# Linear-attention numerators in three head groups instead of four, with inverted gate coefficients and a new instruction order

## The chip, the cores and the metric

The kernel runs on one core of a Trainium2 chip. The core has five engines that run their own instruction streams in order: TensorE (PE, matrix products, with a separate row for its weight loads, PEld), VectorE (DVE), ScalarE (ACT), GpSimd (POOL) and SyncE (SP, which here only issues DMA transfers). Engines wait for one another through semaphores. The metric is the device time of one execution in microseconds (us), as the median of several runs. Products write into PSUM tiles; DVE and ACT read these, POOL works on SBUF alone.

## The reference

One input `x` (2048 rows of 640) goes through two attention layers, A and B, with 32 heads of 20 channels each, and a gate per row mixes them. Everything is in bf16 at the interface.

```python
# A: linear attention; phi(t) = concat(softmax(t), softmax(-t)) over a head's 20 channels
pq = einsum('bhsd,hdf->bhsf', q, w_phi); pk = einsum('bhsd,hdf->bhsf', k, w_phi)
kv = einsum('bhsf,bhsd->bhfd', phi_k, v); z = einsum('bhsf->bhf', phi_k)
num = einsum('bhqf,bhfd->bhqd', phi_q, kv)
den = einsum('bhqf,bhf->bhq', phi_q, z)[..., None] + 1e-06
a = (num / den).reshape(B, S, D) @ wo
# B: four segments of 512 rows; in each, causal softmax attention and a memory M, z of the earlier ones
a_dot = softmax(qs @ ks.T * scale + mask) @ vs
a_mem = (phi(qs) @ M) / (phi(qs) @ z + 1e-06)
o = g * a_mem + (1.0 - g) * a_dot           # g = sigmoid(beta), one per head
M = M + phi(ks).T @ vs; z = z + phi(ks).sum(rows)
b = o_all @ wo_B
# the mix
g = sigmoid((x * gate_w).sum(-1, keepdims=True)); out = g * a + (1 - g) * b
```

Both parts end in a product with 640 x 640 weights, and the gate is one number per row, so the kernel applies the gate to the attention outputs ahead of that product and adds both parts in one accumulation.

## The kernel before

**Tiling.** The 2048 rows are cut into 16 blocks of 128 (a block is the partition dimension) and four segments of 512 rows. The 640 channels are five tiles of 128. Since a head has 20 channels, a tile of 128 rows of a transposed matrix holds 6 or 7 heads and a bit; the tables `H0`, `NH` and `OFF` say which heads touch which of the five tiles.

**PSUM.** One large tile `st4` (four times 512 fp32) holds the attention logits of part B. All other products share four tiles `w` of 512 fp32 a partition. Each use takes a free one (`alloc`), and the last instruction that reads it gives it back (`free`).

**Stages.** The start loads x0 to x3 (the first four row blocks of x), transposes them with PE products (line 681) into `xT` (copied by ACT, line 691, or DVE, line 693) and loads weights. The later blocks of x come by transposing DMAs. Then, for each segment: projections of part B (`seg_in`, line 745: K, Q, V and the gate's logit); K and Q go to DRAM (`kd`, line 764) and come back transposed (`kqT`, line 1109); 20 rounds of logits (line 1138) and one exponential over 128 x 2048 each (line 1144, ACT, tile `PT`), whose diagonal blocks POOL masks (line 1150); products with V (line 1166) and with the memory (line 1185). Part A first goes once over all 16 blocks for its state (`a1`, lines 841 to 867, `kv_pass`, `a1_state`, tile `KVD`). From there on (`switch`, 155 us in the profile) it makes, for each segment, the exponentials of the projected Q with both signs (`a3_pq`, line 988, and the exponentials `Eq`, line 996) and the numerators (`a3_num`). Last, `fin` multiplies both parts' outputs, transposed (`oTA`, `oTB`), with the output weights (line 1086) and stores (`osb`).

**Numerators.** `a3_num(s, qc, hf)` makes half the heads of a row block, in two groups of 8 heads (`PARTS`, indexed by `qt`). A group's products (line 1019) fill 2 x 8 x 22 columns of one tile w: for each sign and head the 20 numerator channels, the product with z (column DH) and the sum of the exponentials (column DH+1, by ones in `KVD`). The two softmaxes are not normalized ahead; with E the numerator, Z its z column and S the sum for either sign, the output is (E1/S1 + E2/S2) / (Z1/S1 + Z2/S2), which is (E1*S2 + E2*S1) / (Z1*S2 + Z2*S1). Six instructions do this, in order: `dz` copies the sums (line 712 on DVE or 710 on ACT), `xx` multiplies Z with the other sign's sum (1032), `rr` adds the two signs (1035) and is inverted (1038), `cs` is the other sign's sum times gate times rr (1040), `ts` scales the numerators (1044) and frees the tile w. Then POOL adds the two signs of a half, 16 heads, into `oA` (1048), and SP stores the row block to DRAM (1054), from where a transposing DMA fetches it for `fin` (1060).

**Output of part B.** `b_out(s, g, ...)` takes four heads' results of a segment. Column DH of the tile w is the denominator; `nx` is 1 in the first segment, where there is no memory part, and 2 in the others. Each part's 16 denominators are inverted (1203) into `rd`, `rd` is multiplied with the coefficients `Cdm` of both parts (1206), and the numerators are scaled by it (1214); POOL adds the parts (1220). `Cdm` is made per segment by POOL (813) from the rows' gates `omgS` (807) and the heads' `omg_b` and `sig_b` (824 to 826).

**Order.** Nothing is scheduled at run time. `ORDER` is a table that lists, for each engine, the numbers of the operations in the order in which the engine gets them; a number is the position at which `op(...)` recorded the operation. (`29*7` stands for 29 to 35.) Operations with two possible engines (`AD`: ACT or DVE, mostly copies out of PSUM) go to the one in whose list they stand. The planner only walks the lists and hands out tiles w; the durations written in `op` serve its walk. `lk=True` marks DVE instructions after which the next POOL instruction gets a wait on that instruction (`run`, "port order").

## Time and profile before

| | us |
|---|---|
| median of 7 runs (lowest 291.19, highest 292.19) | 291.8 |
| the profiled execution | 291.47 |
| its span, first to last instruction | 289.8 |
| PE, ACT, DVE, POOL busy in the span | 281.8, 246.9, 229.3, 188.8 |
| granted TensorE clock | 1.000 |

The busy time by stage, in us:

| stretch | what it mostly holds | PE | DVE | ACT | POOL |
|---|---|---|---|---|---|
| 0 to 20 | loads, transposes, first projections | 18.33 | 9.69 | 8.43 | 8.15 |
| 20 to 40 | projections, first logits | 19.46 | 10.61 | 15.04 | 9.38 |
| 40 to 155 | segments 0 to 2 of B, state of A | 114.77 | 96.12 | 110.24 | 89.58 |
| 155 to 268 | numerators of A, rest of B, output products | 110.50 | 105.12 | 107.75 | 76.66 |
| 268 to 290 | last output products and stores | 18.72 | 7.81 | 5.44 | 4.99 |

PE's busy time counts a product from its start to its modelled end, and products overlap (a 320-column product is shown with 299 ns while the next starts some 136 ns later), so 97% busy is not PE at its peak. The chain of waits is followed back from the last instruction, at each step to what released it. A group of instructions is one line, engine, operation and tile; its row gives the number of instances, the busy time and the mean duration in ns.

### The profile page before, as it was taken

What the parts mean: (1) busy time and instruction counts of PE and PEld (TensorE: products, weight loads), DVE (VectorE), ACT (ScalarE), POOL (GpSimd) and SP (SyncE); (2) the same over time, 40 slices, a digit from 0 to 9 for tenths busy, and PEclk for the clock granted to TensorE, in tenths of its full rate; (3) what the DMA queues carried; (4) which work ended last, traced back from release to release, by engine and by line L of the source; (5) the groups of instructions that cost most, each with busy time, mean ns of one, the idle gap of its engine ahead of it and who ended that gap; (6) DMA issues with size and microseconds to landing.
All of it is one profiled execution on the core that took longest, in us unless ns stands there. A gap on an engine that the chain in (4) does not pass through costs nothing.

```text
span 289.8 us, 9799 instructions
## 1 busy us (share of the span) xinstructions
PE 281.8 (97%) x3764; PEld 192.8 (67%) x3777; DVE 229.3 (79%) x850; ACT 246.9 (85%) x353; POOL 188.8 (65%) x333
## 2 busy tenths in 40 slices
...
GB/s 214 309 214 152 119 248 80 147 106 87 134 42 105 159 102 69 99 57 141 2 125 263 129 181 123 170 79 122 160 171 117 140 105 197 128 100 131 104 106 65
DMA packets 87976, 38.42 MB, mean 133 GB/s; under 512 B 69882, under 2 KB 83834, under 8 KB 87930
## 3 DMA queue, kind: packets, MB, share of 16 engines
...
q10 hardware_dynamic: 656, 0.41, 0.5%
q14 instruction: 17, 0.14, 0.2%
...
## 4 chain that ended last, share of the span: by engine, by line
PE 78%; DVE 14%; DMA 4%; issue 1%; SPq 1%; ACT 1%; POOL 0%; DVEq 0%
PE w L745 34%; PE w L1086 14%; PE w L1166 9%; PE st L1138 7%; PE w L988 4%; DVE ts L1044 4%; PE w L1019 3%; DMA WvA<-in_A_wqkv_dram 2%; PE w L888 2%; DVE cs L1040 2%; PE w L1231 1%; DVE rr L1038 1%; DMA Wc<-in_A_w_phi_dram 1%; DVE tdm L1214 1%; PE w L1185 1%
## 5 line engine op out<-in xcount | busy, mean ns | idle before, releaser
L1144 ACT ACTIVATE PT<-st 128x2048 bf16<-128x2048 f32 x80 | 151.5, 1893 | 4.8 <-PE st L1138 3.8
L1150 POOL TENSOR_SCALAR_AFFINE_SELECT PT<-PT 128x512 bf16<-128x512 bf16 x128 | 79.1, 635 | 42.1 <-ACT PT L1144 13.5
L745 PEld LDWEIGHTS <-xT 128*128 128x128 bf16 x800 | 72.4, 97 | 34.7 <-issue 9.5
L867 POOL TENSOR_TENSOR EkN<-Ek,krec 128x640 bf16<-128x640 bf16 x32 | 40.5, 1273 | 4.6 <-DVE phik L778 1.2
L1166 PEld LDWEIGHTS <-PT 128*128 128x128 bf16 x1280 | 39.8, 96 | 5.3 <-issue 0.8
L1166 PE MATMUL w<-vB,PT 128*128 128x21 bf16 x1280 | 41.5, 172 | 0.1
L745 PE MATMUL w<-WqB,xT 128*128 128x320 bf16 x160 | 36.0, 299 | 0.3 <-ACT kq L710 0.2
L745 PE MATMUL w<-WvA,xT 128*128 128x340 bf16 (+1 forms) x160 | 35.4, 299 | 0.2 <-DMA WvA<-in_A_wqkv_dram 0.2
L745 PE MATMUL w<-WkB,xT 128*128 128x320 bf16 x160 | 34.4, 299 | 0.4 <-DVE xT L693 0.4
L1048 POOL TENSOR_TENSOR oA<-ts 128x320 bf16<-128x320 f32 x32 | 27.4, 862 | 10.9 <-DVE dz L712 3.1
L745 PE MATMUL w<-WkA,xT 128*128 128x320 bf16 x160 | 33.5, 299 | 0.0
L745 PE MATMUL w<-WvB,xT 128*128 128x321 bf16 (+1 forms) x160 | 33.3, 300 | 0.1
L1086 PE MATMUL w<-WoA,oTA 128*128 128x320 bf16 x160 | 32.3, 298 | 0.2
L1086 PE MATMUL w<-WoB,oTB 128*128 128x320 bf16 x160 | 32.3, 299 | 0.0
L1138 PE MATMUL st<-kqT 32*128 32x384 bf16 (+3 forms) x512 | 31.7, 300 | 0.5 <-ACT PT L1144 0.5
L1044 DVE TENSOR_TENSOR ts<-w,cs 128x320 f32<-128x320 f32 x64 | 30.6, 486 | 1.4
L988 PE MATMUL w<-xT,WqA 128*128 128x512 bf16 x87 | 26.7, 378 | 0.8 <-DVE ts L1044 0.2
L1019 PE MATMUL w<-KVD,Eq 128*128 128x88 bf16 (+3 forms) x256 | 26.8, 207 | 0.6
L859 DVE TENSOR_REDUCE ksum<-Ek 128x32 f32<-128x640 bf16 x32 | 25.1, 804 | 2.7 <-ACT Ek L852 2.6
L1220 POOL TENSOR_TENSOR oB<-tdm 128x320 bf16<-128x320 f32 x24 | 20.6, 863 | 7.6 <-DVE dz L712 2.7
L852 ACT ACTIVATE Ek<-w 128x320 bf16<-128x320 f32 x64 | 24.2, 453 | 1.5 <-PE w L745 1.0
L1019 PEld LDWEIGHTS <-Eq 128*128 128x128 bf16 x256 | 19.2, 97 | 9.2 <-issue 2.8
(113 smaller groups left out, 447.7 us busy)
## 6 DMA issues: line engine op xcount, KB each, us to landing
...
```

Of the source, the lines that this page charges most:

```text
L745: nc.tensor.matmul(w[:, 0:width], lhsT=T["xT"][:, c, sc * P:(sc + 1) * P], rhs=T[Wn][:, c, lo:lo + width], start=(c == 0), stop=(c == KC - 1))
L859: op("DVE", 0.74, lambda sgn=sgn: nc.vector.tensor_reduce(out=T["ksum"][js][:, H * sgn:H * sgn + H], in_=T["Ek"][ik][:, sgn].rearrange("p ...
L867: op("POOL", 1.22, lambda sgn=sgn: nc.gpsimd.tensor_tensor(out=T["EkN"][ie][:, 0:2 * D].rearrange("p (h x f) -> p h x f", x=2, f=DH)[:, :, ...
L988: nc.tensor.matmul(w, lhsT=T["WqA"][:, c, t * P:(t + 1) * P], rhs=T["xT"][:, c, s * L:(s + 1) * L], start=(c == 0), stop=(c == KC - 1))
L1019: nc.tensor.matmul(w[:, c0:c0 + m * E2], lhsT=T["Eq"][j][:, sgn, qc * P:(qc + 1) * P], rhs=T["KVD"][:, sgn, OFF[t] + a:OFF[t] + a + m, :]. ...
L1044: op("DVE", dve_t(320), lambda w, c3=c3, qt=qt: nc.vector.tensor_tensor(out=T["ts"][d][:, :, 8 * (qt % 2):8 * (qt % 2) + 8], in0=vw(w)[:, ...
L1048: op("POOL", 0.82, lambda: nc.gpsimd.tensor_tensor(out=T["oA"][o][:, 320 * hf:320 * hf + 320].rearrange("p (h d) -> p h d", d=DH), in0=T[" ...
L1086: nc.tensor.matmul(w[:, 0:320], lhsT=T[nm][j][:, k5, :], rhs=T[Wo][:, k5, hf * 320:hf * 320 + 320], start=(i == 0), stop=(i == 9))
L1138: nc.tensor.matmul(st4[:, i, o:o + w], lhsT=T["kqT"][j][r:r + 32, 0, c * P:(c + 1) * P], rhs=T["kqT"][j][r:r + 32, 1, c * P:L], start=True ...
L1144: op("ACT", act_t(2048), lambda: nc.scalar.activation(out=T["PT"][slot], in_=st4, func=ACT.Exp, scale=SCALE_B), r=("st4",), w=(("PT", slot ...
L1150: nc.gpsimd.affine_select(out=v, in_=v, pattern=[[0, 4], [1, P]], compare_op=ALU.is_ge, fill=0.0, base=0, channel_multiplier=-1)
L1166: nc.tensor.matmul(w[:, j * 84 + i * V1:j * 84 + (i + 1) * V1], lhsT=T["PT"][slot][:, i, o + (j - c) * P:o + (j - c + 1) * P], rhs=T["vB"] ...
```

## The change

- `PARTS` has three groups of 11, 11 and 10 heads (`NHG` = 11). `a3_num` makes groups 0 and 1 with `hf` = 0 and group 2 with `hf` = 1. A group's products fill 484 (or 440) of the 512 columns of a tile w; there are 7 products per sign and row block where there were 8. The six instructions stand once per group. The buffers `dz` to `ts` are three each, one per group; `ts` had two, one per half.
- POOL's addition into `oA` comes after each group, over 11 or 10 heads, not after each half of 16. The store of a row block waits for three additions.
- `omgS`, `omg_b` and `sig_b` become the inverses of what they were, by further reciprocals in `gates` and `beta`, and with them `Cdm`. `b_out` multiplies the denominators in the tile w by `Cdm` first, part by part, and takes one reciprocal over both parts. The multiply no longer carries `lk`.
- `ORDER` is replaced as a whole. On SP the loads of `beta_b` (13) and `Wc` (11) stand right behind the first x block, ahead of the other three; on POOL the mask `m36` (operation 42) stands ahead of the identity (26). The numbers shift, since there are fewer operations.

```diff
@@ ORDER (first lines of each list)
     "PE":
-        "29*7 73*3 77*2 80 88 104 89 82 120 90*2 105 121 92 106 94 122 95 107 123 96 108 124 126 "
...
+        "29*7 73*3 77*2 80 88*2 82 90 104*2 91 106*3 120 92 110*2 121*2 94 112 123*2 113 142 114 "
...
     "ACT":
-        "0 76 79 28 86 101 109 99 133 147 149 197 117 213 229 205 189 175 221 237 187 266 367 431 "
-        "405 510 252 513 245 279 268 287 399 291 315 299 666 843 307 517 379*2 386*2 528 418 411 "
...
+        "0 28 86 79 81 109 93 101 117 125 115 133 147 141 149 131 175 189 163 187 229 237 213 221 "
+        "203 245 235 169 469 259 510 431 463 513 219 197 279 303 283 299 291 205 295 268 307 843 "
...
     "DVE":
-        "27 72 81 70 83 68 93 102 125 134 118 131 135 103 69 115 141 150*2 85 181 190 119 222 238 "
...
+        "27 70 76 87 83 102 72 134 71 68 135 103 99 118 150 119 85 181 190 151 69 191 266*2 252*2 "
...
     "POOL":
-        "26 40 37 39 36 38 42*2 41 44 67 65 47 63*2 62 60 46 45 59 61 48 511 57 56 514*2 518 49 "
...
+        "40 42 26 36*2 43 39 38 41 47 46 64 67 48 61 49 60 45 62 59 57 63 44 511 514 56 515 65 "
...
     "SP":
-        "1*4 5 10 11 13 8 7 6 9 100 132 116 148 12 272 507 273 271 274*2 14 508 220 15*3 541 "
-        "204 667 188 236 542 19 575 18 20 609 576 699 683 22 715 319 21 987 318 610 23 317 991 25 "
...
+        "1 13 11 2*3 10 5 8 7 6 9 116 148 132 100 12 274 507 272*2 271 275 14 508 220 15 541 17 "
+        "16 188 204 667 18 236 542 576 575 19 609 683 699 715 610 319 21 321 987 20 22 320 317 "
...
@@ -806,7 +798,8 @@
             nc.vector.reciprocal(out=gs, in_=gs)
             nc.vector.tensor_scalar(out=og, in0=gs, scalar1=-1.0, scalar2=1.0,
                                     op0=ALU.mult, op1=ALU.add)
-        op("DVE", 0.5, f, w=(("gS", s),), key=key, lk=True)
+            nc.vector.reciprocal(out=og, in_=og)
+        op("DVE", 0.65, f, w=(("gS", s),), key=key, lk=True)
 
         def f2():
             for x, src in enumerate(("omg_b", "sig_b")):
@@ -822,10 +815,11 @@
 
         def f():
             nc.vector.tensor_scalar_add(out=sb_, in0=sb_, scalar1=1.0)
-            nc.vector.reciprocal(out=sb_, in_=sb_)
-            nc.vector.tensor_scalar(out=ob, in0=sb_, scalar1=-1.0, scalar2=1.0,
+            nc.vector.reciprocal(out=ob, in_=sb_)
+            nc.vector.tensor_scalar(out=ob, in0=ob, scalar1=-1.0, scalar2=1.0,
                                     op0=ALU.mult, op1=ALU.add)
-        op("DVE", 0.7, f, w=("sig",), lk=True)
+            nc.vector.reciprocal(out=ob, in_=ob)
+        op("DVE", 0.9, f, w=("sig",), lk=True)
 
 
     EN = [0]
@@ -967,11 +961,11 @@
         tl("WoA", [KC, D], pool=la)
         tl("WoB", [KC, D], pool=la)
         tl("Eq", [2, L], n=NEQ, pool=la)
-        tl("dz", [2, 8], F32, n=3, pool=la)
-        tl("xx", [2, 8], F32, n=3, pool=la)
-        tl("rr", [8], F32, n=3, pool=la)
-        tl("cs", [2, 8], F32, n=3, pool=la)
-        tl("ts", [2, 16, DH], F32, n=2, pool=la)
+        tl("dz", [2, NHG], F32, n=3, pool=la)
+        tl("xx", [2, NHG], F32, n=3, pool=la)
+        tl("rr", [NHG], F32, n=3, pool=la)
+        tl("cs", [2, NHG], F32, n=3, pool=la)
+        tl("ts", [2, NHG, DH], F32, n=3, pool=la)
         tl("oA", [D], n=3, pool=la)
         tl("oTA", [KC, P], n=NOT, pool=la)
         tl("oTB", [KC, P], n=NOT, pool=la)
@@ -997,62 +991,65 @@
                 out=T["Eq"][j][:, sgn], in_=w, func=ACT.Exp, scale=1.0 - 2.0 * sgn),
                w=(("Eq", j, sgn),), key=key, **kw)
 
-    PARTS = (((0, 0, 7), (1, 0, 2)), ((1, 2, 5), (2, 0, 4)), ((2, 4, 4), (3, 0, 5)),
-             ((3, 5, 2), (4, 0, 7)))
+    PARTS = (((0, 0, 7), (1, 0, 5)), ((1, 5, 2), (2, 0, 8), (3, 0, 3)), ((3, 3, 4), (4, 0, 7)))
+    NHG = 11
 
     def a3_num(s, qc, hf, key):
 
 
         key = U(key)
         n = 4 * s + qc
-        d, o = (2 * n + hf) % 2, n % 3
+        o = n % 3
         E2 = DH + 2
-        for qt in (2 * hf, 2 * hf + 1):
+        for q in (2,) if hf else (0, 1):
             bk = bank()
-            c3 = (4 * n + qt) % 3
+            c3, h0 = q, NHG * q
+            nh = min(NHG, H - h0)
+            last = len(PARTS[q]) - 1
             for sgn in range(2):
-                for i, (t, a, m) in enumerate(PARTS[qt]):
+                for i, (t, a, m) in enumerate(PARTS[q]):
                     j = (KC * s + t) % NEQ
 
-                    def f(w, i=i, t=t, a=a, m=m, j=j, sgn=sgn, qt=qt):
-                        c0 = (8 * sgn + H0[t] + a - 8 * qt) * E2
+                    def f(w, i=i, t=t, a=a, m=m, j=j, sgn=sgn, h0=h0, nh=nh, last=last):
+                        c0 = (nh * sgn + H0[t] + a - h0) * E2
                         nc.tensor.matmul(w[:, c0:c0 + m * E2],
                                          lhsT=T["Eq"][j][:, sgn, qc * P:(qc + 1) * P],
                                          rhs=T["KVD"][:, sgn, OFF[t] + a:OFF[t] + a + m, :].rearrange("p h f -> p (h f)"),
-                                         start=(sgn == 0 and i == 0), stop=(i == 1),
+                                         start=(sgn == 0 and i == 0), stop=(i == last),
                                          skip_group_check=True)
                     kw = dict(alloc=bk) if sgn == 0 and i == 0 else dict(use=bk)
                     op("PE", pe_t(m * E2), f, r=(("Eq", j, sgn), ("KVD", sgn), "KVDm"), key=key, **kw)
-            vw = lambda w: w[:, 0:16 * E2].rearrange("p (x h e) -> p x h e", x=2, e=E2)
+            vw = lambda w, nh=nh: w[:, 0:2 * nh * E2].rearrange("p (x h e) -> p x h e", x=2, e=E2)
+            tv = lambda nm, c3=c3, nh=nh: T[nm][c3][:, :, 0:nh]
 
             def small(fn, r, w, dur):
                 op("DVE", dur, fn, r=(bk,) + r, w=w, use=bk, key=key)
-            op(AD, (act_t(16), dve_t(16)), copy_to(lambda w, c3=c3: (T["dz"][c3], vw(w)[:, :, :, DH + 1])),
+            op(AD, (act_t(22), dve_t(22)), copy_to(lambda w, vw=vw, tv=tv: (tv("dz"), vw(w)[:, :, :, DH + 1])),
                r=(bk,), w=(("dz", c3),), use=bk, key=key)
-            small(lambda w, c3=c3: nc.vector.tensor_tensor(
-                out=T["xx"][c3], in0=vw(w)[:, :, :, DH], in1=T["dz"][c3][:, ::-1], op=ALU.mult),
-                (("dz", c3),), (("xx", c3),), 0.1)
-            small(lambda w, c3=c3: nc.vector.tensor_reduce(
-                out=T["rr"][c3], in_=T["xx"][c3].rearrange("p x h -> p h x"), axis=AX.X,
-                op=ALU.add), (("xx", c3),), (("rr", c3),), 0.105)
-            small(lambda w, c3=c3: nc.vector.reciprocal(out=T["rr"][c3], in_=T["rr"][c3]),
-                  (), (("rr", c3),), 0.14)
-            small(lambda w, c3=c3: nc.vector.scalar_tensor_tensor(
-                out=T["cs"][c3], in0=vw(w)[:, ::-1, :, DH + 1], scalar=T["gS"][:, n:n + 1],
-                in1=T["rr"][c3][:, None, :].to_broadcast([P, 2, 8]), op0=ALU.mult, op1=ALU.mult),
-                (("rr", c3), ("gS", s)), (("cs", c3),), 0.155)
-            op("DVE", dve_t(320), lambda w, c3=c3, qt=qt: nc.vector.tensor_tensor(
-                out=T["ts"][d][:, :, 8 * (qt % 2):8 * (qt % 2) + 8], in0=vw(w)[:, :, :, 0:DH],
-                in1=T["cs"][c3][:, :, :, None].to_broadcast([P, 2, 8, DH]), op=ALU.mult),
-               r=(("cs", c3),), w=(("ts", d, qt % 2),), free=bk, key=key)
-        op("POOL", 0.82, lambda: nc.gpsimd.tensor_tensor(
-            out=T["oA"][o][:, 320 * hf:320 * hf + 320].rearrange("p (h d) -> p h d", d=DH),
-            in0=T["ts"][d][:, 0], in1=T["ts"][d][:, 1], op=ALU.add),
-           r=(("ts", d, 0), ("ts", d, 1)), w=(("oA", o, hf),), key=key)
+            small(lambda w, vw=vw, tv=tv: nc.vector.tensor_tensor(
+                out=tv("xx"), in0=vw(w)[:, :, :, DH], in1=tv("dz")[:, ::-1], op=ALU.mult),
+                (("dz", c3),), (("xx", c3),), 0.105)
+            small(lambda w, c3=c3, nh=nh, tv=tv: nc.vector.tensor_reduce(
+                out=T["rr"][c3][:, 0:nh], in_=tv("xx").rearrange("p x h -> p h x"), axis=AX.X,
+                op=ALU.add), (("xx", c3),), (("rr", c3),), 0.11)
+            small(lambda w, c3=c3, nh=nh: nc.vector.reciprocal(out=T["rr"][c3][:, 0:nh], in_=T["rr"][c3][:, 0:nh]),
+                  (), (("rr", c3),), 0.165)
+            small(lambda w, c3=c3, nh=nh, vw=vw, tv=tv: nc.vector.scalar_tensor_tensor(
+                out=tv("cs"), in0=vw(w)[:, ::-1, :, DH + 1], scalar=T["gS"][:, n:n + 1],
+                in1=T["rr"][c3][:, None, 0:nh].to_broadcast([P, 2, nh]), op0=ALU.mult, op1=ALU.mult),
+                (("rr", c3), ("gS", s)), (("cs", c3),), 0.16)
+            op("DVE", dve_t(2 * nh * DH), lambda w, nh=nh, vw=vw, tv=tv: nc.vector.tensor_tensor(
+                out=tv("ts"), in0=vw(w)[:, :, :, 0:DH],
+                in1=tv("cs")[:, :, :, None].to_broadcast([P, 2, nh, DH]), op=ALU.mult),
+               r=(("cs", c3),), w=(("ts", c3),), free=bk, key=key)
+            op("POOL", 0.04 + 0.00244 * nh * DH, lambda h0=h0, nh=nh, tv=tv: nc.gpsimd.tensor_tensor(
+                out=T["oA"][o][:, DH * h0:DH * (h0 + nh)].rearrange("p (h d) -> p h d", d=DH),
+                in0=tv("ts")[:, 0], in1=tv("ts")[:, 1], op=ALU.add),
+               r=(("ts", c3),), w=(("oA", o, q),), key=key)
         if hf:
             rows = slice(qc * P, (qc + 1) * P)
             dma(lambda: nc.sync.dma_start(out=od[s][0][rows, :], in_=T["oA"][o]),
-                (("oA", o, 0), ("oA", o, 1)), (("od", s, 0, qc),), key, 164)
+                tuple(("oA", o, q) for q in range(3)), (("od", s, 0, qc),), key, 164)
 
     def o_get(s, X, qc, key):
         rows = slice(qc * P, (qc + 1) * P)
@@ -1200,14 +1197,13 @@
             return w[:, 0:336].rearrange("p (j i e) -> p j i e", j=4, e=V1)
 
         for x, bk in enumerate(bks):
-            op("DVE", 0.165, lambda w, x=x: nc.vector.reciprocal(
-                out=T["rd"][b][:, x], in_=vw(w)[:, :, :, DH]), r=(bk,), w=(("rd", b, x),),
-               use=bk, key=key)
-        op("DVE", 0.125, lambda w: nc.vector.tensor_tensor(
-            out=T["rd"][b][:, 0:nx], in0=T["rd"][b][:, 0:nx],
-            in1=T["Cdm"][s % 2][:, 0:nx, :, 4 * g:4 * g + 4], op=ALU.mult),
-           r=(("C", s % 2),), w=tuple(("rd", b, x) for x in range(nx)), key=key, lk=True,
-           use=bks[0])
+            op("DVE", 0.1, lambda w, x=x: nc.vector.tensor_tensor(
+                out=T["rd"][b][:, x], in0=vw(w)[:, :, :, DH],
+                in1=T["Cdm"][s % 2][:, x, :, 4 * g:4 * g + 4], op=ALU.mult),
+               r=(bk, ("C", s % 2)), w=(("rd", b, x),), use=bk, key=key)
+        op("DVE", 0.165 if nx == 1 else 0.3, lambda w: nc.vector.reciprocal(
+            out=T["rd"][b][:, 0:nx], in_=T["rd"][b][:, 0:nx]),
+           w=tuple(("rd", b, x) for x in range(nx)), key=key, use=bks[0])
         for x, bk in enumerate(bks):
             def f(w, x=x):
                 dst = oview(s, g) if nx == 1 else T["tdm"][b][:, x]
```

## The prediction

> **What bounds the kernel now.** The page's busy row and its chain were read first.
>
> ```profile
> PE 281.8 (97%) x3764; PEld 192.8 (67%) x3777; DVE 229.3 (79%) x850; ACT 246.9 (85%) x353; POOL 188.8 (65%) x333
> PE 78%; DVE 14%; DMA 4%; issue 1%; SPq 1%; ACT 1%; POOL 0%; DVEq 0%
> ```
>
> The first row says that TensorE is nearly always occupied, the second that the work that ended last was PE's for 78% of the span and VectorE's (DVE) for 14%, some 40 us. The question is where DVE's 40 us lie. The chain asked for 155 to 268 us answers:
>
> ```profile
> by line: PE w L1086 20.6%; PE w L988 10.5%; PE w L1166 9.9%; DVE ts L1044 9.5%; PE w L1019 7.2%; PE st L1138 7.1%; PE w L745 4.7%; DVE cs L1040 4.4%; DVE rr L1038 3.3%; DVE xx L1032 2.8%; DVE rr L1035 2.7%; issue 2.6%; DVE tdm L1214 2.4%; D
> ```
>
> The lines 1032 to 1044 are the numerator groups of part A: five rows with 22.7% of 113 us, 25.7 us. With the copy dz (1.4 us of the chain in 155 to 180, 0.7 in 230 to 255, 0.5 elsewhere) and what the rounding of shares leaves, adding up the pieces of the chain stage by stage gives 12.6, 1.3, 2.4, 6.3 and 6.5 us in the five stages below, 29.1 in all: 11.2 for ts, 17.9 for the small instructions. Before 155 us the chain is nearly all PE's. Then the busy time by stage (columns: the stretch; its length; busy us and instructions of PE, PE's weight loads, DVE, ACT, POOL; granted clock; DMA share; GB/s):
>
> ```profile
> 40.00:155.00 115.00, 114.77 (x1676) 80.02 (x1675) 96.12 (x262) 110.24 (x169) 89.58 (x141) 1.00 0.51 102
> 155.00:180.00 25.00, 24.11 (x333) 15.07 (x335) 23.31 (x107) 24.83 (x32) 15.80 (x25) 1.00 0.73 179
> 180.00:205.00 25.00, 24.89 (x385) 17.16 (x384) 22.62 (x100) 23.17 (x27) 14.64 (x22) 1.00 0.55 122
> 205.00:230.00 25.00, 24.79 (x364) 16.48 (x366) 22.62 (x104) 24.19 (x31) 17.63 (x27) 1.00 0.72 151
> 230.00:255.00 25.00, 24.23 (x341) 16.17 (x343) 24.07 (x124) 24.75 (x32) 17.42 (x25) 1.00 0.68 139
> 255.00:268.00 13.00, 12.47 (x198) 9.13 (x197) 12.50 (x68) 10.81 (x12) 11.18 (x17) 1.00 0.55 116
> ```
>
> The reader is to see two things: DVE is over 90% busy from 155 to 268, and ScalarE (ACT) is just as full: it has 0.17, 1.83, 0.81, 0.25 and 2.19 us to spare, 5.25 in all. What DVE gives back, ACT lets through only that far. After 268 only PE is busy, with output products.
>
> **Numerator groups.** The price of a group, from the groups of instructions (instances, busy us, mean ns):
>
> ```profile
> L1044 DVE TENSOR_TENSOR ts<-w,cs 128x320 f32<-128x320 f32 x64 | 30.6, 486 | 1.4
> L1040 DVE SCALAR_TENSOR_TENSOR cs<-w,gS,rr 128x16 f32<-128x16 f32 x64 | 14.2, 230 | 0.6
> L1038 DVE RECIPROCAL rr<-rr 128x8 f32<-128x8 f32 x64 | 12.2, 198 | 0.6
> L712 DVE COPY dz<-w 128x16 f32<-128x16 f32 x56 | 9.0, 167 | 1.2 <-PE w L1019 1.0
> ```
>
> With xx at 169 and the sum rr at 163 ns the five small ones take 167+169+163+198+230 = 927 ns, and 64 groups 59.3 us. Larger forms by the nearest rows: the addition into KVa took 404 ns for 240 elements and 587 for 420, 1.02 ns an element, so ts over 440 elements costs 608, over 400 567. Reciprocals of 8 and 16 took 198 and 239, 5.1 an element: 213 for 11, 208 for 10. The copies of 16 and 40 elements (167 and 190) give 1 ns an element: six more elements cost 6 ns each in dz, xx, the sum and cs. A new group's small ones are then 965 ns; 48 groups take 46.3 us, a factor of 0.781. ts goes from 64 x 486 = 31.1 to 32 x 608 + 16 x 567 = 28.5, a factor of 0.916. In instruction durations DVE loses 15.6 us.
>
> On the path it is less. The timeline of DVE, where two groups run together:
>
> ```profile
> 173.01 0.25 DVE L712 COPY dz<-w 128x16 f32<-128x16 f32 x2
> 173.21 0.26 DVE L1032 TENSOR_TENSOR xx<-w,dz 128x16 f32<-128x16 f32 x2
> 173.42 0.25 DVE L1035 TENSOR_REDUCE rr<-xx 128x8 f32<-128x16 f32 x2
> 174.21 0.89 DVE L1044 TENSOR_TENSOR ts<-w,cs 128x320 f32<-128x320 f32 x2
> ```
>
> Two copies of 167 ns end within 250 ns: an independent instruction starts before the one ahead has ended, so a removed one is not worth its whole duration. I therefore scale what the chain holds: 17.9 x 0.219 + 11.2 x 0.084 = 4.9 us (by stage 2.2, 0.15, 0.4, 1.1, 1.0). The Trainium skill's page "VectorE: DVE Perf Modes", section "The DRAIN you can't avoid", says that after every DVE operation the next waits until the pipeline has emptied, and advises fewer operations; by that alone all 15.6 us would go from a full DVE. The rows just shown overlap, so the rule's sum is not used.
>
> What is late next is ACT. If a stage can't shrink by more than ACT's spare time in it, 0.17 + 0.15 + 0.4 + 0.25 + 1.0 = 2.0 us are left. The new order also takes work from ACT: counting its rows between the 46th and the last PT exponential, four osb copies (431 ns), five dz (176) and one kq (444) go, three vB (432) and one eq (654) come: 1.1 us less. I take 3.1 us. Ends: 2.0 and 4.9.
>
> **PE, banks and POOL.** A quarter filled 352 of a w tile's 512 columns, a third fills 484; the columns of part A stay, 32 matmuls (44 columns, 184 ns) and weight loads go: 0. A w tile is held longer by 122+38 ns of DVE work and 132 more columns, but for 48 groups rather than 64; that is inside the factors. POOL's addition oA has rows at 320 elements (862 ns) and, as Cdm, at 128 (399): 2.4 ns an element, so 48 additions of 621 and 573 take 29.0 us against 27.6. POOL is 65% busy, which covers it; the chain passes one oA (0.85) and one mask (0.60) at 258 to 260, so an addition more ahead of a mask costs 0.6. Taken: 0; ends -0.6 and +0.6. Behind each addition wait the masks of PT, and behind these the products L1166.
>
> **b_out.** Before: two reciprocals of 16 from w (239 each) and a multiply of 32 (212), 690 ns, 24 times; 239+246 eight times. After: two multiplies reading w (as xx: 169) and a reciprocal of 32 (as krec: 337), 675; or 169+239. Taken: 0, as the chain holds 1.1 us of L1203 in the whole stage. New is that the first instruction, not the second, needs Cdm. For the last segment POOL makes it from 221.3 to 222.0 and the first reciprocal that belongs to it starts at 223.7: 1.7 us of cover, and without it DVE and the w tile wait by as much as Cdm is late. POOL waited 5.9 us in all for the old multiply (masks 3.3, oA 1.2, EkN 0.8, zh 0.6), off the path: 0, and -0.6 where the mask at 259 was meant. The page "SBUF — State Buffer", section "SBUF: two separate sides", says that a DVE operation with two SBUF inputs and a GpSimd operation that reads SBUF exclude each other; the multiply did spread from 161 to 494 ns, so the rule would credit up to 0.3 us for each of 32, beside work that the chain does not hold. The gates' five more reciprocals (four of 178, one of 353) cost 1.1 us of DVE off the path: 0, unless Cdm's cover is gone.
>
> **The start.**
>
> ```profile
> 3.64 3.76 DMA Wc<-in_A_w_phi_dram
> 7.50 0.30 DVE WphiD L667
> 7.80 0.41 DVE xT L693
> 8.26 5.49 PE w L745 x39
> ```
>
> DVE stands still for Wc until 7.5, and x2's and x3's copies are queued behind it; PE's stream starts at 8.26 after three single products at 7.0. The new SP order issues beta and Wc right behind x0 (issues of 0.34 and 0.40 us: x1 to x3, gw, WqB, WvB and all behind them on SP come 0.85 later at most), and gives POOL the mask m36 (2.25 us) and one pad (0.42) before the identity, which comes at 4.1 rather than 1.4, 0.7 after x0's landing at 3.4. x3's transposes, last at 7.85 now, then end near the same time, but the products find x0's and x1's copies ready: full stream at about 7.8 with two products done rather than three: -0.3. Ends: -0.5 (Wc early at no cost) and +0.85 (all loads later, nothing won). WvA, issued behind the kd stores (14.61, landing 21.3), moves with them.
>
> **The order.** The number and kind of PE's products before each exponential hardly differ. On ACT copies move: 13.4 us instead of 11.2 before the first PT exponential, 34.1 instead of 31.9 from there to the ninth (kq, vB, WkA), 123.5 instead of 126.7 from there to the 46th (vA to DVE). ACT was busy for 8.4 of the first 20 us and 15.0 of the next 20, which covers the first two. Taken: 0. Ends: -2.1, the one clear excursion of the chain from PE to DVE before 155 (128.7 to 131.2: rd 0.38, tdm 0.81, WqA 0.90), and +4.4, the moved copies uncovered.
>
> **Sum.** The profiled execution took 291.47 us (span 289.8 and 1.7 around it); 291.47 - 3.1 - 0.3 = 288.1. The median of the seven runs, 291.8, lies 0.3 above that execution: 288.4.
>
> **Rivals.** (a) ACT caps the stage hard and nothing is won at the start: 291.8 - 2.0 + 0.85 = 290.7; with POOL's 0.6 291.3, within 0.2% of before, about what a measurement of this kernel can tell from no change. For it: 24.83 of 25 and 24.75 of 25 on ACT. Against: 2.19 spare where DVE holds half the chain. (b) Slower: the copies that ACT takes over before the ninth exponential make the exponentials late, and PE, whose order is fixed, waits. Place: up to 55 us; price up to 4.4; it decides from 3.1 + 0.3 + 0.6 = 4.0 upward with the forecast's gain, from 2.6 with the capped one. 291.8 + 4.4 - 2.0 = 294.2 at the far end, 293.0 for 3.2. For it: ACT 19.84 of 20 busy in 40 to 60. Against: ACT's 16 idle us before 40. (c) ACT does not cap, since its copies can go to the relieved DVE: 291.8 - 4.9 - 0.3 = 286.6, with the excursion at 130 gone 284.5. (d) The change does nothing to the path, because PE is the bound and DVE's pieces hide behind PE: 291.8. Against: PE's busy time is short by 0.9, 0.8 and 0.5 us in just the stages where DVE holds most.
>
> **How the numbers follow.** Forecast 0.50, (c) 0.19, (a) and (d) together 0.13, of which 0.05 ends faster, (b) 0.18. Faster by over 0.2%: 0.50 + 0.19 + 0.05 = 0.74, less 0.04 for the forecast's own upper end (+0.85 +0.6 +...), which falls inside the band: 0.70. Within 0.2%: 0.08 + 0.03 = 0.11. Slower: 0.18 + 0.01 = 0.19. The range takes in (c) to 285.2 and (b) to 293.2; the forecast's own is 286.5 to 290.7.
>
> **What would show it.** Right: 48 ts of about 600 ns; DVE's share of the chain in the last third down by a sixth or more; ACT at 98% there; DVE's first WphiD before 5.5 and PE's stream from about 7.8; the ninth exponential no later than 55. Wrong: the ninth exponential late; ts or oA on the chain more than before; DVE waiting for Cdm in the last segment.

## The result and the profile after

The changed kernel takes 290.88 us (median of 14 runs, 289.99 to 291.35) beside 291.78 for the kernel before on the same chip; the ratio is 0.9967, 95% interval [0.9958, 0.9977]. It is faster, by 0.33%; 0.9 us came where 3.4 were forecast. The profiled execution took 290.86 us with a span of 289.1. The page's busy row and the shares of its chain:

```profile
PE 280.7 (97%) x3733; PEld 191.6 (66%) x3745; DVE 223.3 (77%) x766; ACT 248.0 (86%) x346; POOL 191.6 (66%) x349
PE 73%; DVE 17%; ACT 3%; DMA 3%; issue 2%; DVEq 0%; ACTq 0%
```

VectorE's share of the chain went up, from 14% to 17%, though it has 84 instructions fewer. The chain from 155 to 268 us:

```profile
by line: DVE ts L1041 12.6%; PE w L1083 10.5%; PE w L737 9.5%; PE w L982 7.8%; PE w L1163 6.7%; PE st L1135 5.3%; issue 5.1%; PE w L1015 4.7%; DVE cs L1037 4.6%; DVE tdm L1210 3.8%; DVE rr L1035 3.6%; ACT PT L1141 3.4%; DVE rr L1032 3.0%; D
```

The line ts (1041) now heads it. By the five stages the numerator groups hold 3.2, 0.9, 13.0, 9.3 and 7.0 us of the chain, 33.4 in all, where they held 29.1 (a piece that crosses a border counts in both stages; split at the borders it is 33.2 and 28.5). The busy time by stage (columns as in the prediction):

```profile
155.00:180.00 25.00, 24.72 (x344) 15.49 (x344) 22.95 (x94) 24.95 (x30) 17.15 (x28) 1.00 0.79 182
180.00:205.00 25.00, 24.86 (x354) 16.49 (x354) 21.60 (x81) 22.10 (x27) 15.77 (x26) 1.00 0.65 138
205.00:230.00 25.00, 24.43 (x350) 15.82 (x352) 22.33 (x91) 24.27 (x29) 16.72 (x28) 1.00 0.65 144
230.00:255.00 25.00, 23.94 (x330) 16.00 (x332) 22.81 (x102) 24.11 (x29) 18.32 (x29) 1.00 0.54 112
255.00:268.00 13.00, 12.58 (x195) 9.27 (x193) 12.46 (x59) 11.10 (x11) 11.29 (x19) 1.00 0.55 133
```

The number behind a stretch's length is TensorE's busy time. From 155 to 268 us PE stands idle for 2.5 us here, and for 2.5 us in the kernel before (0.89, 0.11, 0.21, 0.77 and 0.53 by the rows that the prediction shows). Both records lack some matmuls (3733 of 3745 are there here), so the true idle time may be somewhat less: it is 1.8 in wq_early below, whose record is complete. On the other hand this count lets a product last until its modelled end, so waits that are shorter than the overlap of two products do not show in it. The prices of the operations came out as forecast:

```profile
L1041 DVE TENSOR_TENSOR ts<-w,cs 128x440 f32<-128x440 f32 x32 | 19.3, 612 | 1.4
L1041 DVE TENSOR_TENSOR ts<-w,cs 128x400 f32<-128x400 f32 x16 | 9.2, 573 | 0.8
L1204 DVE RECIPROCAL rd<-rd 128x32 f32<-128x32 f32 x24 | 8.4, 352 | 0.7
L1037 DVE SCALAR_TENSOR_TENSOR cs<-w,gS,rr 128x22 f32<-128x22 f32 x32 | 7.4, 238 | 0.5
L1035 DVE RECIPROCAL rr<-rr 128x11 f32<-128x11 f32 x32 | 6.8, 218 | 0.5
```

The most useful comparison is by marks that all kernels share: the starts (us) of the 80 large exponentials of PT (128x2048), here a few, from the timelines of the profiled executions. Experiments are named below.

| kernel | 1st | 41st | 49th | 57th | 73rd | 80th | span | median |
|---|---|---|---|---|---|---|---|---|
| before | 25.7 | 153.6 | 176.7 | 200.5 | 247.1 | 266.4 | 289.8 | 291.78 |
| after | 25.8 | 152.6 | 175.5 | 198.3 | 246.9 | 265.5 | 289.1 | 290.88 |
| t3_old | 25.8 | 153.7 | 176.8 | 201.5 | 249.6 | 268.9 | 292.7 | 294.45 |
| bout_old | 26.4 | 154.2 | 177.4 | 201.2 | 248.6 | 268.7 | 292.1 | 293.45 |
| early_new | 25.4 | 156.7 | 182.0 | 205.9 | 252.8 | 272.1 | 295.4 | 297.06 |
| early_new_bout | 25.6 | 152.4 | 177.1 | 200.9 | 248.1 | 268.4 | 291.8 | 293.14 |
| t3_new_boutold | 25.9 | 157.3 | 180.1 | 203.2 | 251.9 | 270.5 | 294.6 | 296.33 |
| wq_early | 25.4 | 152.2 | 175.0 | 197.9 | 246.4 | 265.0 | 288.6 | 290.33 |
| after_dve | 25.7 | 152.5 | 175.3 | 198.0 | 245.4 | 264.0 | 287.5 | 289.60 |
| before_dve | 25.5 | 153.5 | 176.6 | 200.4 | 246.8 | 265.9 | 289.2 | 291.18 |
| after_act | 26.4 | 153.3 | 176.0 | 198.9 | 246.6 | 265.6 | 289.2 | 290.59 |
| after_pe | 26.3 | 153.1 | 176.0 | 198.6 | 246.9 | 265.3 | 286.3 | 287.97 |

The changed kernel gains nothing at the start, is 1.0 us ahead at the 41st, where the numerator groups (first product at 160.2 us in both kernels) have not begun, 2.2 ahead at the 57th, and only 0.2 at the 73rd. Where both kernels work on the groups, from the 41st to the 80th exponential, the changed one takes 112.9 us and the kernel before 112.8. So two questions: what wins before the groups, and what eats the groups' gain.

### The profile page after: what moved, and what is told of

It is laid out like the page before. It is cut to its first block, busy times and chain, and to the rows that moved or that the text cites. A ratio compares the mean times of both kernels' runs of the same rounds, so it can differ in the third digit from the quotient of the medians.

```text
span 289.1 us, 9662 instructions
## 1 busy us (share of the span) xinstructions
PE 280.7 (97%) x3733; PEld 191.6 (66%) x3745; DVE 223.3 (77%) x766; ACT 248.0 (86%) x346; POOL 191.6 (66%) x349
## 4 chain that ended last, share of the span: by engine, by line
PE 73%; DVE 17%; ACT 3%; DMA 3%; issue 2%; DVEq 0%; ACTq 0%
PE w L737 38%; PE w L1083 9%; PE w L1163 8%; PE st L1135 7%; DVE ts L1041 5%; PE w L982 3%; PE w L882 2%; ACT PT L1141 2%; PE w L1015 2%; DVE cs L1037 2%; DMA WqB<-in_B_wq_dram 2%; DVE tdm L1210 1%; DVE rr L1035 1%; PE w L1227 1%; DMA WkB<-in_B_wk_dram 1%
## 5 line engine op out<-in xcount | busy, mean ns | idle before, releaser
L1163 PEld LDWEIGHTS <-PT 128*128 128x128 bf16 x1280 | 40.7, 96 | 5.9 <-issue 2.1
L1163 PE MATMUL w<-vB,PT 128*128 128x21 bf16 x1280 | 43.1, 172 | 0.0
L737 PE MATMUL w<-WvB,xT 128*128 128x320 bf16 (+1 forms) x160 | 37.0, 300 | 0.0
L737 PE MATMUL w<-WkB,xT 128*128 128x320 bf16 x160 | 36.6, 299 | 0.1
L1045 POOL TENSOR_TENSOR oA<-ts 128x220 bf16<-128x220 f32 (+1 forms) x48 | 30.3, 638 | 9.5 <-DVE ts L1041 4.8
L737 PE MATMUL w<-WvA,xT 128*128 128x340 bf16 (+1 forms) x160 | 33.4, 299 | 0.1
L1083 PE MATMUL w<-WoA,oTA 128*128 128x320 bf16 x160 | 31.4, 298 | 0.4 <-DVE ts L1041 0.2
L1041 DVE TENSOR_TENSOR ts<-w,cs 128x440 f32<-128x440 f32 (+1 forms) x48 | 28.4, 599 | 2.2
L982 PE MATMUL w<-xT,WqA 128*128 128x512 bf16 x88 | 25.8, 379 | 1.2 <-DVE ts L1041 0.6
L1015 PE MATMUL w<-KVD,Eq 128*128 128x154 bf16 (+5 forms) x224 | 25.0, 213 | 0.3
L1210 DVE TENSOR_TENSOR tdm<-w,rd 128x320 f32<-128x320 f32 x48 | 21.6, 485 | 0.9
```

The source lines that it names most:

```text
L737: nc.tensor.matmul(w[:, 0:width], lhsT=T["xT"][:, c, sc * P:(sc + 1) * P], rhs=T[Wn][:, c, lo:lo + width], start=(c == 0), stop=(c == KC - 1))
L982: nc.tensor.matmul(w, lhsT=T["WqA"][:, c, t * P:(t + 1) * P], rhs=T["xT"][:, c, s * L:(s + 1) * L], start=(c == 0), stop=(c == KC - 1))
L1015: nc.tensor.matmul(w[:, c0:c0 + m * E2], lhsT=T["Eq"][j][:, sgn, qc * P:(qc + 1) * P], rhs=T["KVD"][:, sgn, OFF[t] + a:OFF[t] + a + m, :]. ...
L1041: op("DVE", dve_t(2 * nh * DH), lambda w, nh=nh, vw=vw, tv=tv: nc.vector.tensor_tensor(out=tv("ts"), in0=vw(w)[:, :, :, 0:DH], in1=tv("cs" ...
L1045: op("POOL", 0.04 + 0.00244 * nh * DH, lambda h0=h0, nh=nh, tv=tv: nc.gpsimd.tensor_tensor(out=T["oA"][o][:, DH * h0:DH * (h0 + nh)].rearr ...
L1083: nc.tensor.matmul(w[:, 0:320], lhsT=T[nm][j][:, k5, :], rhs=T[Wo][:, k5, hf * 320:hf * 320 + 320], start=(i == 0), stop=(i == 9))
```

## Experiments

Each experiment was timed beside runs of the kernel before, whose medians are 291.50 to 291.67 us; the ratios, with 95% intervals, are to these.

**The parts on the old table.** Three kernels keep the old table's places. A group of three takes the place of an old quarter, step for step (first where quarter 0 stood, second where 2 stood, third where 3 stood; in the last row block of a segment the second stands where quarter 1 stood); POOL's additions stand where the old ones stood.

```diff
 # t3bout_old: the changed kernel; t3_old: gates and b_out as before. PE's list, around the first group
-1681*5 1688*5 1709 1168 2054 1710*3 2475 1713 2476 1716 2477 1717
+1168 1684*2 1688*5 2054 2475*5 1709 1716 1710 1717*3 1711*2 2489 1713
 # bout_old: the kernel before, with gates(), beta() and b_out() of the changed one
```

> All of the change's operations (three groups, the inverted gate coefficients, one reciprocal for both parts), but in the places of the old table: each engine's list is the old one, a group of three put where the half of quarter that began there stood (first third where the first quarter stood, second third where the third quarter stood, last third where the last quarter stood); x3 stays where it was. Theory 'the groups give the gain, and the new table takes part of it back after 190 us': faster than the changed kernel, 288 to 290 us. Theory 'VectorE's dependent chains pace the last third whatever the order': 290.5 to 291.5. Theory 'the gain is the table's, the cheaper groups are worth nothing': at or above the kernel before, 291.5 to 293.

> The three groups alone on the old table; gate coefficients, denominators and their reciprocals as before. It tells the groups from the denominators' part. My prediction put the second at nothing (690 ns of denominators against 675): so the same as the run with both parts on the old table within 0.4 us. If the one reciprocal for both parts matters (one longer wait for two banks in place of two short ones), it stands 0.5 us or more away from that run.

> The kernel before with the inverted gate coefficients and the one reciprocal alone, on the old table and with quarters. By my prediction 0, so 291.5 to 292.0 us. If holding two banks until the later one is there costs PE, up to +1 us; if the shorter chain behind the denominators helps, down to -0.5.

Measured: t3bout_old 294.82 us, ratio [1.0095, 1.0137]; t3_old 294.45, [1.0080, 1.0109]; bout_old 293.45, [1.0050, 1.0077]. t3_old came within 0.4 us of t3bout_old, as expected; the other two are slower than any theory had them. Each part alone, on the old table, is a loss, and together they are hardly worse than the groups alone. On the old table, then, the groups bring no gain. In bout_old 0.7 us are lost before the first exponential, where two loads (Wc, WvA) landed later in this execution (t3bout_old has the same gates and 25.7), and 1.6 between the 57th and the 80th. In t3_old 2.4 are lost between the 49th and the 80th. PE's longest waits in t3_old from 155 us on:

```profile
PE st L1134 <- ACT PT L1140: 1.9, 6, 0.4
PE w L1014 <- DVE ts L1040: 0.6, 2, 0.3
PE w L1082 <- DVE tdm L1210: 0.5, 2, 0.3
```

(The numbers are us in total, times, longest us.) Six waits for exponentials that come late, each of 0.4 us at most: a list of places made for one set of durations, run with another, leaks in many small pieces. One of the pieces is the old denominators' multiply: from 171 us on it takes 341 to 750 ns seven times in t3_old, beside a GpSimd operation each time, and its 32 instances take 9.7 us where they took 7.1 in the kernel before. It is not the whole of the loss, for t3bout_old has no such multiply and is as slow. These three runs price the parts together with the misfit, and can't separate the two.

**The new table without the groups.**

```diff
 # early_new: the kernel before; every op that the new table ends ahead of the first numerator
 # matmul is issued in the new order, the rest in the old; SP: 1 13 11 2*4 10 8 ... as in wq_early
 # early_new_bout: the same with gates(), beta() and b_out() of the changed kernel
 # early_new_nolk: early_new with
-           r=(("C", s % 2),), w=tuple(("rd", b, x) for x in range(nx)), key=key, lk=True,
+           r=(("C", s % 2),), w=tuple(("rd", b, x) for x in range(nx)), key=key,
 # t3_new_boutold: the changed kernel with gates(), beta() and b_out() of before
```

> None of the changed operations: the kernel before with its quarters, gates and denominators, in which only the places up to the first numerator matmul are the new table's (x3 behind x2 too, and the first half of WqB ahead of the gate rows as in the run before); from the first numerator on, every engine's list is the old one. In the traces the changed kernel is 1.3 us ahead at the 49th large exponential (176 us), before the groups of three can have given anything. Theory 'the gain is the table's early part': 289.6 to 290.4 us (291.6 less 1.3 less 0.4 of WqB). Theory 'what is won early is lost again at whatever paces the last third': 291.3 to 291.8.

> The run with the new table's early part (5.4 us slower than before, with the old denominators), now with the inverted gate coefficients and the one reciprocal; still quarters, still the old list from the first numerator on. In that run the old multiply, both operands in SBUF, took up to 1.18 us where it met an operation of GpSimd, and each time the next product on PE came later. Theory 'the new table's places suit only the new denominators, whose multiply reads PSUM': the 5.3 us lost up to 166 us are gone, and 290.5 to 291.5 us are left (the old list's late part costs 1.2 with the new denominators). If it stays above 295, the multiply is not the cause.

> The changed kernel with the gate coefficients and denominators of before, on the new table with the groups of three. By the same theory 4 to 7 us slower than the changed kernel (295 to 298), with single multiplies of 0.5 to 1.2 us. If the denominators are worth nothing, as my prediction had it: 290.5 to 291.3.

> The run with the new table's early part and the old denominators (297.1 us), less one thing: GpSimd's next operation is no longer ordered behind the denominators' multiply (no data passes between them). If GpSimd's wait for the multiply is what cost there: 293 to 294 us, as with the new denominators. If the multiply's own stretch on VectorE is the cost, and the order was a protection: 296.5 to 298, and multiplies of up to 1.2 us as before.

Measured: early_new 297.06 us, ratio [1.0166, 1.0201], a miss by 7 us: it is 5.3 behind at the 49th exponential, and 5.0 of that come after the ninth. (Its expectation takes the groups of three to have given nothing by the 49th; in the changed kernel six ts have started by then, so the 41st is the safer mark.) early_new_bout 293.14, [1.0035, 1.0066], is 1.6 above its expected range: 3.9 us of the loss are gone, and at the 41st exponential it is 1.2 ahead of before, as the changed kernel is with 1.0. At the seam to the old list it loses 1.5 by the 49th, and 1.6 more between the 57th and the 80th, where bout_old loses as much. t3_new_boutold 296.33, [1.0151, 1.0181], and early_new_nolk 296.98, [1.0172, 1.0242], came as expected by the theory of the multiply. The timelines of early_new on POOL, DVE and PE show one of the losses:

```profile
70.48 1.27 POOL L866 TENSOR_TENSOR EkN<-Ek,krec 128x640 bf16<-128x640 bf16 x1
70.34 0.25 DVE L1202 RECIPROCAL rd<-w 128x16 f32<-128x16 f32 x1
70.62 1.16 DVE L1205 TENSOR_TENSOR rd<-rd,Cdm 128x16 f32<-128x16 f32 x1
71.82 0.49 DVE L1213 TENSOR_TENSOR oB<-w,rd 128x320 bf16<-128x320 f32 x1
72.36 0.30 PE L744 MATMUL w<-WvA,xT 128*128 128x340 bf16 x1 [0.83 <-DVE oB L1213]
```

The old multiply of 16 elements, both operands in SBUF, starts 0.14 us behind POOL's EkN and ends 0.03 after it: 1.16 us where its least is 0.17. The output that frees the w tile is late, and PE stands for 0.83 us. Ten of the 32 multiplies of early_new take over 300 ns, and each of the ten ends 0.03 to 0.05 us after a GpSimd operation; all 32 take 12.4 us, against 7.1 in the kernel before. The tile rd in early_new, early_new_nolk and early_new_bout (ns: least, median, most; first and last start), each line from its own kernel:

```profile
L1205 DVE TENSOR_TENSOR rd<-rd,Cdm x32: 174/192/1183, 43.8 to 278.1; 128x32 f32<-128x32 f32 x24, 128x16 f32<-128x16 f32 x8
```

```profile
L1205 DVE TENSOR_TENSOR rd<-rd,Cdm x32: 176/193/1180, 43.8 to 277.8; 128x32 f32<-128x32 f32 x24, 128x16 f32<-128x16 f32 x8
```

```profile
L1204 DVE TENSOR_TENSOR rd<-w,Cdm x56: 111/165/175, 43.8 to 273.9; 128x16 f32<-128x16 f32 x56
```

The new multiply reads one operand from w, which is in PSUM, and never takes more than 175 ns. Dropping only the order that lets POOL wait for the multiply changes nothing (297.0), so POOL's wait is not the loss; the multiply's own stretch is what stays. The Trainium skill's page "SBUF — State Buffer", section "SBUF: two separate sides", says that a VectorE operation with two SBUF inputs and a GpSimd operation that reads SBUF exclude each other; the run agrees, with 1.16 us beside a POOL operation of 1.27. In the old table POOL's operations stood so that the old multiply took 494 ns at most; the new table does not keep them apart, and with the new denominators it need not. On the new table they are worth 296.33 - 290.88 = 5.4 us (5.7 if each is compared with its own runs of before), 4.5 of them by the 41st exponential. From the first to the 41st, ahead of all numerator groups, the profiled executions take, in us:

| | old denominators | new denominators |
|---|---|---|
| old table | 127.9 (before, t3_old) | 127.8 (bout_old, t3bout_old) |
| new table | 131.3, 131.4 (t3_new_boutold, early_new) | 126.8 (after, early_new_bout, wq_early) |

This answers the first question: the 1.1 us come of the new order and the new denominators together. Neither has them alone, and the groups have no part in them.

**What one engine's work is worth.** Five kernels leave part of the computation out, as their expectations say; a step set to None is planned in its place but issues nothing.

```diff
 # after_dve (before_dve: the same on the quarters)
-            small(lambda w, ...: nc.vector.tensor_tensor(out=tv("xx"), ...
-            small(lambda w, ...: nc.vector.tensor_reduce(out=T["rr"][c3][:, 0:nh], ...
+            small(None, (("dz", c3),), (("xx", c3),), 0.105)
+            small(None, (("xx", c3),), (("rr", c3),), 0.11)
-            ... nc.vector.reciprocal(out=T["rr"][c3][:, 0:nh], in_=T["rr"][c3][:, 0:nh])
+            ... nc.vector.reciprocal(out=T["rr"][c3][:, 0:nh], in_=tv("dz")[:, 0])
 # after_act (after_dveact: both edits)
-            op("ACT", act_t(512, False), lambda: nc.scalar.activation(out=T["eq"][e], ...
+            op("ACT", act_t(512, False), None, ...
-                out=T["phiq"][f], in0=T["phiq"][f], in1=T["eq"][e], op=ALU.min),
+                out=T["phiq"][f], in0=T["phiq"][f], in1=T["phiq"][f], op=ALU.min),
 # after_pe
-                    op("PE", pe_t(320), f, ...
+                    op("PE", pe_t(320), f if k5 < 4 else None, ...
```

> The changed kernel without the product and the reduction over the two parts in every group (the reciprocal reads the copied denominators' first part instead; the numbers of the numerators are then not the reference's): 48 x (175 + 170) ns, 16.5 us of VectorE, and two links of each group's chain less. It prices VectorE's work in the numerator groups, about as much as the change took away (15.6 us). By the step of my prediction (the share of this work that lies on the chain of waits, 0.42 in this kernel): 5 to 7 us faster than the changed kernel. Theory 'ScalarE, 24.1 to 25.0 of 25 us in these stages, holds the pace': 0 to 2 us. Theory 'VectorE's chains hold 203 to 242 us': 2.5 to 4.

> The same as the run without product and reduction, made from the kernel before: 64 groups, about 22 us of VectorE, on the old table. By the step of my prediction (17.9 of 59.3 us of these small operations on the chain, so 0.30 of it): 6 to 7 us faster than the kernel before, or 2 to 3 with ScalarE's spare time as the cap. If work of VectorE is not what the time is made of, 0 to 1.5.

> The changed kernel without the 24 exponentials of the queries (128x512, 0.65 us each: 15.6 us of ScalarE, from the second sequence block on; the minimum on VectorE reads its own tile twice; the linear part's denominators are then not the reference's). It prices ScalarE's work. Theory 'ScalarE holds the pace': 4 us or more faster than the changed kernel. Theory 'VectorE's chains hold it': 0 to 2 us.

> The changed kernel with both reliefs at once: without product and reduction in the numerator groups (16.5 us of VectorE) and without the queries' 24 exponentials (15.6 us of ScalarE); the output is not the reference's. If the two engines take turns, so that relieving one alone shows the other: 5 us or more faster than the changed kernel. If TensorE is the bound: 1.3 to 2.5 us.

> The changed kernel without the last of the five chunks of each of the two output products (64 matmuls of 320 columns between 188 and 285 us, 142 ns apart in the traces: 9.1 us of TensorE; the output is then not the reference's). It prices TensorE's work beside the runs that priced VectorE's (16.5 us less, 1.3 us of time) and ScalarE's (15.6 us less, 0.3). Theory 'TensorE's fixed list is the bound and the other engines only fill its few gaps': 6 to 9 us faster than the changed kernel. Theory 'VectorE and ScalarE hold the last third together': 0 to 3 us.

| left out | us of it | median | gain | gain per us |
|---|---|---|---|---|
| before_dve: DVE | 21 | 291.18 (before: 291.64) | 0.46 | 0.02 |
| after_dve: DVE | 16.5 | 289.60 (after: 290.88) | 1.28 | 0.08 |
| after_act: ACT | 15.6 | 290.59 | 0.29 | 0.02 |
| after_dveact: both | 32.1 | 289.31 | 1.57 | 0.05 |
| after_pe: PE | 9.1 | 287.97 | 2.91 | 0.32 |

The changed kernel and these were timed beside different runs of before, whose medians differ by 0.3 us at most (291.50 to 291.78); a gain like after_act's 0.29 can't be told from none. This is the centre of the study. In the kernel before, the change's whole saving on DVE and more could be taken away for 0.46 us, ratio [0.9972, 1.0000]. With ScalarE relieved as well (after_dveact) the relief of VectorE brings 1.57 instead of 1.28, so ScalarE is not what caps it. All these prices hold for lists of places that were not made anew for the shorter work. Two stages of before_dve, to be laid beside those of before:

```profile
155.00:180.00 25.00, 23.79 (x337) 15.01 (x340) 21.13 (x84) 24.83 (x32) 15.87 (x25) 1.00 0.72 180
230.00:255.00 25.00, 24.15 (x342) 16.21 (x343) 21.79 (x91) 24.84 (x32) 17.80 (x25) 1.00 0.61 137
```

DVE falls from 23.31 to 21.13 and from 24.07 to 21.79; PE stays at 24. With VectorE's links gone the chain goes over to PE's. The chain from 188 to 268 us in the changed kernel, in after_dve and in after_pe:

```profile
by line: DVE ts L1041 16.2%; PE w L1083 14.8%; issue 6.2%; DVE cs L1037 5.9%; PE w L1163 5.0%; ACT PT L1141 4.8%; DVE rr L1035 4.5%; DVE xx L1029 3.8%; PE st L1135 3.8%; DVE rr L1032 3.8%; DVE tdm L1210 3.6%; PE w L737 3.3%; DVE dz L704 3.2
```

```profile
by line: PE w L1079 29.0%; PE w L1159 9.5%; PE st L1131 8.1%; PE w L1015 7.9%; PE w L982 7.7%; ACT Eq L990 5.3%; issue 5.2%; ACT PT L1137 4.8%; PE w L737 4.0%; POOL PT L1143 3.2%; POOL oA L1041 3.1%; DVE ts L1037 2.3%; DVE tdm L1206 2.2%; P
```

```profile
by line: DVE ts L1041 14.0%; issue 9.5%; PE w L1083 7.0%; POOL PT L1147 6.0%; DVE cs L1037 5.0%; ACT PT L1141 4.7%; PE w L1163 4.0%; DVE rr L1035 4.0%; POOL oA L1045 3.9%; DMA oTA<-od 3.5%; DVE xx L1029 3.4%; DVE rr L1032 3.3%; ACT eq L1111
```

In after_dve ts falls from 16.2% of this stretch to 2.3%, and 1.3 us come of it. In after_pe PE's products fall and DVE, POOL, ACT and a DMA stand there instead. Its 2.9 us are mostly the last stretch, where PE alone works: the output products from about 275 us on take 8.01 us of the chain instead of 10.15, so 2.1 us come from 16 of the 64 matmuls, and less than 1 from the 48 before. The two last expectations point in opposite directions: after_dveact came as for "TensorE is the bound", after_pe as for "VectorE and ScalarE hold the last third together". So neither holds it alone. From the first to the 80th exponential, the relief of VectorE brings 1.4 us, that of ScalarE 0.6, both 1.9, and that of PE 0.7: where one engine's work goes, the chain goes over to the others, which were hardly behind. How near they are to one another stays open, for no run relieves PE together with VectorE, and none relieves GpSimd.

**The start.**

```diff
 # wq_early, SP's list
-1 13 11 2*3 10 5 8 7 6 9
+1 13 11 2*4 10 8 7 6 9
```

> The changed kernel with one load moved on SP: the first half of Wq's second operand (WqB) is issued ahead of the gate rows, right behind x3. In the changed kernel's profile PE starts its stream 0.6 us earlier but waits 0.58 us for WqB, and the first exponential is no earlier than before. If WqB's load is the limit there: 0.3 to 0.6 us faster than the changed kernel, PE's wait in front of the first WqB matmul gone. If the next loads, or ScalarE's first copies, take the place: the same as the changed kernel within 0.2 us. If the gate rows, now later, hold the first gates: slower, up to 0.5 us.

Measured 290.33 us, ratio to before [0.9945, 0.9974], 0.55 below the changed kernel, or 0.34 if each is compared with its own runs of before; the intervals of the two ratios overlap, so a gain over the changed kernel is not shown. PE's timeline in the changed kernel, whose first WphiD started at 5.91 and whose stream begins at 7.64:

```profile
7.64 1.39 PE L737 MATMUL w<-WkB,xT 128*128 128x320 bf16 x9
9.61 0.45 PE L737 MATMUL w<-WqB,xT 128*128 128x320 bf16 x2 [0.58 <-DMA WqB<-in_B_wq_dram]
```

and in wq_early:

```profile
7.97 1.39 PE L740 MATMUL w<-WkB,xT 128*128 128x320 bf16 x9
9.19 0.43 PE L740 MATMUL w<-WqB,xT 128*128 128x320 bf16 x2
```

The wait is gone; PE's stream starts 0.33 later in this execution and is still 0.4 ahead at every exponential from the first on, and 0.5 in the span; executions of one kernel's loads differ by up to 0.7 there, as told below. It has the lowest median here of the kernels that compute the whole.

**Two that missed.**

```diff
 # q_new: the new table and denominators with quarters (third's places 0, 1, 2 -> quarters 0, 1, 2+3)
-            c3 = (4 * n + qt) % 3
+            c3 = qt            # four sets of dz, xx, rr, cs, ts
 # best2: wq_early, and in DVE's list
-2585 2598 2586 2587 2599 2588 2600 2589 2590 2601*3
+2585*3 2598 2588*2 2599 2590 2600*4
```

> The new table and the new denominators with quarters in place of groups of three: the first quarter stands where the first third stood, the second where the second stood, the third and the fourth together where the last third stood, step by step in turn; four sets of the small tiles and of ts, so that no quarter waits for the one before. SP as in the changed kernel. It is the counterpart of the run with the groups on the old table. If the groups save what my prediction said (VectorE 15.6 us in durations, 3 us of time): 293 to 295 us. If only order and denominators count: 290.3 to 291.5.

> The run with WqB earlier, and one more edit: at 232.7 us VectorE runs the first group's six steps before the second's instead of in turn, so that the ts for which PE waits 0.59 us at 234.6 starts about 0.25 us earlier. If PE's waits are what the time is made of: 0.2 to 0.3 us faster than that run (290.1). If the next wait takes it: the same, 290.3.

q_new took 311.11 us, far beyond either expectation. The largest of PE's waits:

```profile
PE w L1022 <- DVE ts L1047: 6.2, 11, 1.4
```

At the products of a quarter PE waits eleven times, 6.2 us in all, for a ts, the instruction that frees a w tile. PE is idle for 12.6 us from 155 to 268 us, against 2.5 in the changed kernel. That the fourth quarter takes a tile which the table's places do not provide for is argued from this, and the run says nothing of the groups: what groups of three are worth on the table made for them stays open.

best2 took 290.81 us, ratio [0.9955, 0.9995], no gain over wq_early: PE's wait in front of WqA at 235 is still 0.6. VectorE's timeline tells why, first wq_early, then best2 (the first group's dz and the ts for which PE waits):

```profile
232.68 0.27 DVE L707 COPY dz<-w 128x22 f32<-128x22 f32 x2 [0.24 <-issue]
233.93 0.62 DVE L1044 TENSOR_TENSOR ts<-w,cs 128x440 f32<-128x440 f32 x1
```

```profile
232.87 0.18 DVE L707 COPY dz<-w 128x22 f32<-128x22 f32 x1 [0.26 <-issue]
234.12 0.62 DVE L1044 TENSOR_TENSOR ts<-w,cs 128x440 f32<-128x440 f32 x1
```

From dz to ts it is 1.25 us both times, with the second group's steps in between or behind. They had run in time that the first group's own chain of steps leaves free, so moving them away could bring nothing.

## Why the prediction was wrong

**Numerator groups: -3.1, the step that failed.** The prices were right: five small ones at 967 ns for 11 heads (forecast 965), ts at 612 and 573 (608 and 567), 15.3 us less in durations (15.6), 14.4 of them on VectorE, since some dz stand on ScalarE. The wrong term is the conversion, 17.9 x 0.219 + 11.2 x 0.084 = 4.9, which takes VectorE's share of the chain as the price of its work: 0.31 us of time for each us of DVE. The runs give 0.02 on the kernel before and 0.08 on the changed one. The chain names one path; beside it ran others that were hardly shorter. A mark for this stood in the prediction: PE idle for 0.9, 0.8 and 0.5 us "in just the stages where DVE holds most". It was used as an argument against rival (d), that PE is the bound. No relief of VectorE or ScalarE in these runs brought more than PE's 2.5 us of idle time; that this time is the ceiling is argued, for in before_dve it did not shrink (3.1 us from 155 to 268).

**ACT as the cap: wrong.** 15.6 us taken from ScalarE gave 0.3, and taken together with VectorE's 16.5 they added 0.3 to VectorE's 1.3. ACT's spare time by stage, from which the 3.1 was made, did not bound the gain. With both relieved PE holds over 70% of the chain from 155 to 268 us; without PE's chunk it is the others'.

**Where the groups' gain went.** From the 57th to the 73rd exponential (198 to 247 us) the changed kernel gives back 2.1 us of its lead. With VectorE relieved it gives back 0.9 (2.53 ahead at the 57th, 1.67 at the 73rd). So 1.2 of the 2.1 hang on VectorE, which has 13.0 us of chain in the stage from 205 to 230, and PE's two waits there are for ts, 0.20 at 218 and 0.61 at 235. Why the new order leaves VectorE's groups on the path there, no run shows. The timeline of DVE shows what a group costs when no other runs beside it:

```profile
207.34 0.18 DVE L1029 TENSOR_TENSOR xx<-w,dz 128x20 f32<-128x20 f32 x1
207.55 0.17 DVE L1032 TENSOR_REDUCE rr<-xx 128x10 f32<-128x20 f32 x1
207.76 0.22 DVE L1035 RECIPROCAL rr<-rr 128x10 f32<-128x10 f32 x1
208.01 0.24 DVE L1037 SCALAR_TENSOR_TENSOR cs<-w,gS,rr 128x20 f32<-128x20 f32 x1
208.28 0.57 DVE L1041 TENSOR_TENSOR ts<-w,cs 128x400 f32<-128x400 f32 x1
```

Each step starts 20 to 40 ns after the one ahead has ended; a pair overlaps (two copies of 167 ns within 250, in the prediction), and in best2 and wq_early a second group's steps cost the first none of its time. So a removed step takes less from VectorE's busy time than from its durations: in before_dve 21.1 us of durations went and the busy time fell from 229.3 to 218.2. In the changed kernel VectorE's durations fell by 13.3 us in all and its busy time by 6.0. The Trainium skill's page "VectorE: DVE Perf Modes", section "The DRAIN you can't avoid", says that the next operation does not start until the pipeline has emptied, but adds that one that is not held starts earlier; the rows here show both, the dependent steps the first and the pairs the second. What holds an operation no run here tests.

**b_out: 0, wrong by size.** The price was right (2 x 166 + 352 = 684 ns, forecast 675), but the place was not: on the new table the new denominators are worth 5.4 us, on the old one they cost 1.9. The prediction had the mechanism, the multiply's spread from 161 to 494 ns, and credited up to 0.3 us for each "beside work that the chain does not hold". In a new order the old multiply's spread reached 1183 ns and PE waited behind it. DVE waited for Cdm nowhere: POOL had made the last by 213.7 us, where it made it until 222.0 before.

**The order: 0 (ends -2.1 and +4.4).** Inside the ends, and wrong as a term of its own: with the new denominators the order brings 1.0 us between the first exponential and the 41st (126.8 against 127.8), without them it costs 3.4. ScalarE's moved copies made no exponential late (the ninth at 55.4, before 55.3).

**The start: -0.3, measured 0.** PE's stream began 0.6 us earlier, and WqB, issued later on SP, took 0.58 back.

**Rivals and signs.** The direction held by luck: what was won was won ahead of the groups, by the order and the denominators, which the prediction had at 0 each, and from the 41st to the 80th exponential, where the groups were to bring 3.1 us, nothing came (112.9 against 112.8). Rival (a) at 290.7, the cap with nothing won at the start, came nearest by its number, but its reason, ScalarE as the cap, is refuted. Rival (d), that DVE's pieces hide behind PE, is nearer to what the relief of VectorE shows, but PE's own relief shows that PE is not the bound alone. Two of the signs of being right came, 48 ts at 612 and 573 ns and PE's stream at 7.64. The others failed: the numerator groups' part of the chain rose from 29.1 to 33.4 us instead of falling by a sixth; ACT is at 94% in the five stages, not 98%; the first WphiD came at 5.91, not before 5.5; the ninth exponential at 55.4, not 55. Of the signs of being wrong, "ts or oA on the chain more than before" came with ts; the wait for Cdm did not.
